# Two of the channel mixing's three parts run during attention instead of one (decaying attention, token and channel mixing, gated convolution; one core)

## The chip, the cores and the metric

The kernel runs on one core of a Trainium2 chip. The metric is the device time of one launch in microseconds: the median of three runs of the kernel before is 717.75 us (716.49 to 718.46). TensorE is called PE here, VectorE DVE, ScalarE ACT, GpSimd POOL and SyncE, which issues the DMAs, SP.

## The reference

Three networks follow one another on 4 batches of 576 positions. The first is causal attention with a decay (8 heads of 64 per batch, 32 heads in all), the second mixes along the positions (token mixing) and then along the channels (channel mixing), the third is a gated convolution.

```python
scores = where(causal, -1e9, q @ k.T / sqrt(64) + decay)     # per head
x = concat_heads(softmax(scores) @ v)                        # [4, 576, 512]
u = x + (relu(x.T @ w_tok1) @ w_tok2).T                      # token mixing, 576 -> 256 -> 576
x2 = u + relu(u @ w_ch1) @ w_ch2                             # channel mixing, 512 -> 1536 -> 512
h = relu(x2 @ w_in)                                          # 512 -> 1024
out = (h * sigmoid(conv3(h))) @ w_out
```

## The kernel before

Every large product is made of three fp16 products: each operand is a high and a low half, and `mm3` (lines 279 to 284) issues high by high, high by low and low by high, so lines 282, 283 and 284 carry nearly all of PE's work. The channel mixing works on 8 chunks of 288 columns, two per batch. Its inner 1536 channels are 12 blocks of 128, called m. For each m, `m1` (w_ch1 by the halves `uh`, `ul` of u) fills a PSUM bank, `rh` on ACT and `rl` on DVE (lines 662 and 666, tile `r`) take it out as two halves, and `m2` (w_ch2 by `r`) sums over m into one bank per output block d.

The 12 blocks are dealt into parts, `PARTS_M = (5, 4, 3)`. The first `EARLY` parts are computed during attention: as soon as a batch's two token mixings are done, part 0 of its two chunks runs, its sum is scaled by ACT (line 682) into the tile `res`, and SP stores it to the DRAM array `p_d`. The other parts run after attention: `mix_input` loads the chunk's halves, u and the stored sum, POOL adds u to the sum (line 739), and DVE adds each later part's bank onto it (line 678).

Weights come as 64-bit numbers. A block goes through the two tiles `wraw`: SP loads it, ACT shifts it (line 319), DVE joins it (lines 323 and 324, the decode), ACT squares it for its size (line 520). A spread on PE (line 262) brings the sizes of a set to all partitions, DVE makes a power of two of them (`pw`), and the set is then split into halves. For an early set `ONP` says by whom: with 2 POOL does it all (line 555 scales, line 274 casts the high half, line 277 makes the low half), with 1 POOL scales and makes the low half and ACT casts, with 0 ACT makes the high half (line 570) and DVE the low one (line 574). Before, w_ch1's part 0 has 2 and w_ch2's part 0 has 0. The sets are called c10 and c20 (w_ch1 and w_ch2 of part 0), c11 and c21 (part 1), c12 and c22 (part 2).

Heads 8 to 30 make the probabilities' halves on POOL (`ph`, line 1037) and DVE (`pl`, line 1043), and a DMA turns each. `pv` multiplies them by v (lines 1098 to 1100; 1093 for the first eight heads), `xh` and `xl` are the halves of a head's result, `t1` and `t2` are the token mixing of four heads. `um` is the size of a batch's u, `su` the power of two made of it, and `ul` (line 613) the low halves that the first m1 needs. Banks of the tag w (four of them) serve spreads, pv, t1, t2, m1 and the early m2.

The order of all this is made on the host: `Order` (line 19) holds tasks with an engine, a duration, a rank, the data they read and write and the banks they take. It always issues what can start first, and of those the lowest rank. The tasks are then emitted in that order, so each engine, SP's queue included, has a fixed program. The early channel mixing has the last rank on PE (`LATE`), so it fills what attention leaves.

Of the kernel before, what the change touches and what calls it, by code (L numbers as in the profile page):

```python
# [8 lines left out]
F32 = mybir.dt.float32  # L9
# [10 lines left out]
class Order:  # L20
# [3 lines left out]
    LAG = {"PE": 0.25, "DVE": 0.12, "ACT": 0.2, "POOL": 0.12, "SP": 0.0, "-": 0.0}  # L24

# [34 lines left out]
    def run(self):  # L60
# [35 lines left out]
        for _ in range(n):  # L96
            best = None
            for e, ks in open_.items():
                if not ks:
                    continue  # L100
                at = free[e] if e != "-" else 0.0
                pick = None
                for k in ks:
                    r = ready[k]
                    if takes[k]:
                        r = max(r, slot(k))
                    if r >= far:
                        continue
                    c = (max(r, at), self.tasks[k][2], k)
                    if pick is None or c < pick:  # L110
                        pick = c
                if pick and (best is None or pick[0] < best[0]):
                    best = (pick[0], pick[2], e)
# [30 lines left out]
def fox_moe_kernel(  # L144
# [14 lines left out]
    nc = tc.nc  # L159
# [51 lines left out]
    XHP = 8  # L211
    ONP, TONP = (2, 0), (1, 1)
    SETR = ((-20.0, 0.0),)
    LATER = (-30.0, 10.0, 30.0)
# [9 lines left out]
    p_d = dram.tile([KD, 128, NT], F32, name="p_d")  # L224
# [418 lines left out]
    def channel_mix(c, part, rank, u_of, p_of, rts, tag, tag2, pe, evac):  # L643
# [40 lines left out]
        def store(d):  # L684
            nc.sync.dma_start(p_d[d, :, c * CH:(c + 1) * CH], box["res", d])
# [12 lines left out]
        for d in range(KD):  # L698
# [14 lines left out]
            T("SP", 0.4, rank + evac, store, d, reads=[kd], writes=[("p_d", c, d)], moved=0.7)  # L713

    def mix_input(c, rank):
# [18 lines left out]
        def load_p():  # L734
            box["p"] = pools["p2a"].tile([128, KD, CH], F32, tag="p", name="p", bufs=PB)
            nc.sync.dma_start(box["p"], p_d[:, :, cols].rearrange("k p s -> p k s"))
# [7 lines left out]
        T("SP", 0.4, rank - 2, load_p, reads=[("p2a",)] + [("p_d", c, d) for d in range(KD)],  # L744
          writes=[(kp, d) for d in range(KD)], moved=2.8)
        T("SP", 0.4, rank - 2, load_u, reads=[("u_d", c, 0), ("u_d", c, 1), ("p2a",)], writes=[ku], moved=2.8)
        for d in range(KD):
            T("POOL", 0.86, rank, add_u, d, reads=[ku], writes=[(kp, d)])
        return (r, kv), (box, kp)
# [17 lines left out]
    with tc.manual_schedule():  # L767
# [277 lines left out]

        def pt_of(n):
# [98 lines left out]
        def pair(p):  # L1145
# [19 lines left out]
            for n in (2 * p, 2 * p + 1):  # L1165
# [17 lines left out]
                else:  # L1183
# [5 lines left out]
                    for q in range(2):  # L1189
                        T("DVE", (1.35, 0.9)[q], rank + 4, lo_part, n, q,  # L1190
# [6 lines left out]
                for i in ORDER:  # L1197
                    T("PE", (0.22 if n < FULL else 0.1) * len(PVB[i]), rank + 6, pv, n, i, reads=[*kp, *vk], writes=[kw, ("xf", g % 2, n % HG)],
                      pools=["a3"], ring=[kw])
                T("DVE", 0.5, rank + 6, norm, n, reads=[kw, ("vsc", g % 3)], writes=[("rs", n % 2)], pools=A1, ring=[kw])  # L1200
                T("DVE", 0.46, rank + 6, xout, n, reads=[kw, ("rs", n % 2)], writes=[("xf", g % 2, n % HG)], pools=A1, ring=[kw])
                T("POOL" if n < XHP else "ACT", 0.47, rank + 6, x_hi, n, reads=[("xf", g % 2, n % HG)], writes=[("xh", n % HG)], pools=A1)
                T("POOL", 1.05, rank + 6, x_lo, n, reads=[("xf", g % 2, n % HG), ("xh", n % HG)],
# [90 lines left out]
        def group(g):  # L1294
            t0 = (HG * g + HG - 1) * PER + 6
# [59 lines left out]
        AVAIL = [(H * (b + 1) - 1) * PER + 30 for b in range(B)]  # L1355
# [31 lines left out]
        for g in range(NG):  # L1387
# [242 lines left out]
```

## Time and profile before

| | |
|---|---|
| median of three runs | 717.75 us |
| the profiled execution | 717.09 us, span 715.3 us |
| PE busy | 693.4 us (97%) |
| DVE, ACT, POOL busy | 501.8, 429.7, 266.2 us |

The busy time of an engine is the union of its instructions. PE is busy nearly everywhere, so what is left to win is its idle time, and the views that list it are the busy time by stretches and the timeline of PE with the idle time that stands ahead of an instruction. Attention lasts until about 300 us, the late channel mixing until about 500 us, and the gated convolution follows.

### The profile page before, as it was taken

The page shows a single profiled execution, that of the slowest core. Times are in us where ns is not written, and L with a number is a line of the kernel's source. Part 1 is how long each engine was busy: PE and PEld are TensorE (multiplying, and loading weights), DVE is VectorE, ACT ScalarE, POOL GpSimd, SP SyncE. Part 2 cuts the span into 40 slices and gives each one's busy share as a digit, 9 for nine tenths or more (in the row PEclk, how much of TensorE's full clock was granted, in tenths as well). Part 3 has the DMA queues.
Part 4 walks back from the last instruction along what each step waited for, and adds up shares of the span by engine and source line. Part 5 has one row for each costly group of instructions (what it writes and reads, how often), then busy time and mean ns, then how long its engine had stood idle before and what let it go on. Part 6 is the DMA issues. An engine that isn't in the chain of part 4 may idle for free.

```text
span 715.3 us, 16400 instructions
## 1 busy us (share of the span) xinstructions
PE 693.4 (97%) x6417; PEld 559.4 (78%) x6417; DVE 501.8 (70%) x1255; ACT 429.7 (60%) x942; POOL 266.2 (37%) x344
## 2 busy tenths in 40 slices
PE   7999897799999999999999999999999999999998
PEld 6888676587778787887888778778878778778786
DVE  5778989998876788436666856635778866875570
ACT  5777886576845685555674544312177766676671
POOL 2145898657682867230000222102023222323240
PEclk9999999999999999999999999999999999999999
DMA  9435899799995987875454855345211121100101
GB/s 203 148 93 176 212 275 186 143 249 244 231 225 123 220 165 178 220 256 157 151 180 124 284 187 164 100 134 160 66 42 58 51 59 35 57 20 26 34 18 51
DMA packets 152974, 101.99 MB, mean 143 GB/s; under 512 B 89984, under 2 KB 145024, under 8 KB 152896
## 3 DMA queue, kind: packets, MB, share of 16 engines
q1 hardware_dynamic: 152896, 100.94, 54.6%
q8 instruction: 50, 0.82, 0.5%
q14 instruction: 28, 0.23, 0.1%
HBM read 57.73 MB, written 23.59 MB: 114 GB/s over the span
## 4 chain that ended last, share of the span: by engine, by line
PE 82%; DVE 7%; POOL 5%; ACT 2%; issue 2%; DMA 1%; SPq 0%; DVEq 0%; POOLq 0%; ACTq 0%
PE w L282 14%; PE w L283 14%; PE w L284 14%; PE z L283 8%; PE z L282 8%; PE z L284 8%; PE z L1004 5%; PE w L1093 3%; PE w L1245 2%; POOL vp L916 2%; PE z L1008 1%; POOL vp L274 1%; DVE pl L1043 1%; ACT t L1028 1%; PE w L1099 1%
## 5 line engine op out<-in xcount | busy, mean ns | idle before, releaser
L284 PEld LDWEIGHTS <-w 128*128 128x128 f16 x1280 | 125.3, 98 | 34.9 <-DVE w L574 3.2
L282 PEld LDWEIGHTS <-w 128*128 128x128 f16 x1280 | 124.9, 98 | 34.4 <-issue 2.7
L283 PEld LDWEIGHTS <-w 128*128 128x128 f16 x1280 | 125.0, 98 | 34.3 <-issue 3.5
L282 PE MATMUL w<-uh,w 128*128 128x288 f16 x416 | 119.0, 286 | 1.2 <-DVE r L666 1.2
L284 PE MATMUL w<-uh,w 128*128 128x288 f16 x416 | 119.0, 286 | 0.0
L283 PE MATMUL w<-ul,w 128*128 128x288 f16 x416 | 119.0, 286 | 0.0
L277 POOL TENSOR_TENSOR g<-sg,g 128x286 f16<-128x286 f32 (+1 forms) x64 | 55.1, 867 | 150.2 <-ACT g L271 148.5
L1530 DVE SCALAR_TENSOR_TENSOR cv<-hp,cw,cv 128x286 f32<-128x286 f32 (+1 forms) x128 | 75.1, 594 | 38.2 <-ACT cv L1524 36.0
L662 ACT ACTIVATE r<-w 128x288 f16<-128x288 f32 x96 | 39.2, 408 | 87.9 <-PE w L284 87.7
L1028 ACT ACTIVATE t<-t,m 128x576 f32<-128x576 f32 (+4 forms) x160 | 81.3, 552 | 17.3 <-DVE m L1022 17.2
L739 POOL TENSOR_TENSOR p<-p,u 128x288 f32<-128x288 f32 x32 | 27.3, 883 | 150.1 <-DVE wraw L323 78.1
L1022 DVE CUSTOM_DVE_ANT_0 t<-z,mask 128x576 f32<-128x576 f32 (+4 forms) x160 | 69.9, 478 | 11.1 <-PE z L1008 11.0
L666 DVE SCALAR_TENSOR_TENSOR r<-w,r 128x288 f16<-128x288 f32 x96 | 43.4, 453 | 47.4 <-ACT r L662 46.6
L283 PE MATMUL z<-g,w 128*128 128x286 f16 (+1 forms) x256 | 73.3, 286 | 0.0
L282 PE MATMUL z<-g,w 128*128 128x286 f16 (+1 forms) x256 | 73.0, 285 | 0.0
L284 PE MATMUL z<-g,w 128*128 128x286 f16 (+1 forms) x256 | 72.9, 285 | 0.0
L284 PE MATMUL w<-vh,w 128*128 128x288 f16 x224 | 64.1, 286 | 0.0
L282 PE MATMUL z<-r,w 128*128 128x288 f16 x224 | 64.1, 286 | 0.0
L283 PE MATMUL w<-vl,w 128*128 128x288 f16 x224 | 64.1, 286 | 0.0
L284 PE MATMUL z<-r,w 128*128 128x288 f16 x224 | 64.1, 286 | 0.0
L282 PE MATMUL w<-vh,w 128*128 128x288 f16 x224 | 64.1, 286 | 0.0
L283 PE MATMUL z<-r,w 128*128 128x288 f16 x224 | 64.1, 286 | 0.0
(206 smaller groups left out, 1699.8 us busy)
## 6 DMA issues: line engine op xcount, KB each, us to landing
wraw<-in_moe_w_ch_dram SPq DMA_DIRECT2D x24, 512.0 KB, 4.7
qk<-in_qk_dram SPq DMA_DIRECT2D x16, 608.0 KB, 5.1
u_d<-us SPq DMA_DIRECT2D x8, 576.0 KB, 4.5
p_d<-res SPq DMA_DIRECT2D x32, 144.0 KB, 3.6
p<-p_d SPq DMA_DIRECT2D x8, 576.0 KB, 5.4
u<-u_d SPq DMA_DIRECT2D x8, 576.0 KB, 4.9
x_d<-p SPq DMA_DIRECT2D x8, 576.0 KB, 3.4
u<-x_d SPq DMA_DIRECT2D x8, 576.0 KB, 3.9
```

What stands on the lines that cost most here:

```text
L277: nc.gpsimd.tensor_tensor(o, a, b, ALU.subtract)
L282: nc.tensor.matmul(ps, wh, xh, start=(first and i == 0), stop=False)
L283: nc.tensor.matmul(ps, wh, xl, start=False, stop=False)
L284: nc.tensor.matmul(ps, wl, xh, start=False, stop=(last and i == n - 1))
L662: nc.scalar.activation(out=t[:, 0, :], in_=box["z", m], func=AF.Relu)
L666: nc.vector.scalar_tensor_tensor(t[:, 1, :], box["z", m], 0.0, f32(t[:, 0, :]), ALU.max, ALU.subtract)
L739: nc.gpsimd.tensor_tensor(box["p"][:, d], box["p"][:, d], box["u"][:, d], ALU.add)
L1004: nc.tensor.matmul(out_[x], t[r, Q0[i]:Q0[i] + 128], t[r, k0:k0 + n], start=first, stop=False)
L1022: nc.vector.tensor_tensor_reduce(to, z_t.pop((n, i)), mk, -0.125, 3e38, ALU.add, ALU.min, m_t[n][0:rows, i:i + 1])
L1028: nc.scalar.activation(out=tt[0:rows, o:o + w], in_=tt[0:rows, o:o + w], func=AF.Exp, bias=m_t[n][0:rows, i:i + 1], scale=-1.0)
L1093: nc.tensor.matmul(o[:, 0:65], p32(n)[:, 128 * blk:128 * blk + 128], vp32_t[g % 2][:, slot, hh, :], start=(j == 0), stop=(j == nb - 1))
L1530: nc.vector.scalar_tensor_tensor(cv, hp_t[m][:, s0 + t:s1 + t], cw[:, t, m:m + 1], cv, ALU.mult, ALU.add)
```

## The change

`PARTS_M` becomes (4, 4, 4) and `EARLY` 2. Parts 0 and 1 of a batch now both run during attention, with ranks 14 apart per chunk, each with its own DRAM array, `p_d[0]` and `p_d[1]`. After attention a third load, `more`, brings the second sum, and POOL adds it in 4 further instructions per chunk. Two further 2 KB weight tiles are kept from the start (NE 17). c11 and c21 are split during attention as the early sets are, c12 and c22 afterwards. Who splits changes: c10 and c11 have 1 (POOL scales and makes low, ACT casts), c20 and c21 have 2 (all on POOL). The token weights' first set is cast by POOL instead of ACT, and so are the high halves of heads 8 to 11 (`XHP`). Ranks of the sets move (`SETR`, `LATER`, `AVAIL`). `WAIT` is 0 for every engine, `REST` is 0, `RG` is 0 and `RN`, `RL`, `RP` are the ranks that stood there before, so the planner's rule and the two new functions for a head's low half change nothing by themselves. In the changed file the helper lines are 8 higher (282 to 284 become 290 to 292) and later ones 20 to 40.

```diff
-    PARTS_M = (5, 4, 3)
-    EARLY = 1
+    PARTS_M = (4, 4, 4)
+    EARLY = 2
-    NE = 15
+    NE = max(15, 2 * M1 + 1)
-    XHP = 8
-    ONP, TONP = (2, 0), (1, 1)
-    SETR = ((-20.0, 0.0),)
-    LATER = (-30.0, 10.0, 30.0)
+    XHP = 12
+    ONP, TONP = (1, 2), (2, 1)
+    SETR = ((0.0, 0.0),)
+    SETR += ((0.0, 45.0),)
+    LATER = (-60.0, 20.0, 40.0)
-    p_d = dram.tile([KD, 128, NT], F32, name="p_d")
+    p_d = [dram.tile([KD, 128, NT], F32, name=f"p_d{x}") for x in range(EARLY)]
...
-            nc.sync.dma_start(p_d[d, :, c * CH:(c + 1) * CH], box["res", d])
+            nc.sync.dma_start(p_d[part][d, :, c * CH:(c + 1) * CH], box["res", d])
...
+        def load_more(x):
+            box["more"] = pools["p2a"].tile([128, KD, CH], F32, tag="more", name="more", bufs=1)
+            nc.sync.dma_start(box["more"], p_d[x][:, :, cols].rearrange("k p s -> p k s"))
+
+        def add_more(d):
+            nc.gpsimd.tensor_tensor(box["p"][:, d], box["p"][:, d], box["more"][:, d], ALU.add)
...
-    AVAIL = [(H * (b + 1) - 1) * PER + 30 for b in range(B)]
+    AVAIL = [(H * (b + 1) - 1) * PER + 20 for b in range(B)]
...
-                for e in range(2):
-                    channel_mix(2 * b + e, 0, AVAIL[b] + e * 14, early_u[2 * b + e], None, rts1, "w", "w", LATE, -20.0)
+                for x in range(EARLY):
+                    for e in range(2):
+                        channel_mix(2 * b + e, x, AVAIL[b] + (e + 2 * x) * 14, early_u[2 * b + e], None, rts1, "w", "w", LATE,
+                                    -20.0)
```

The fixed programs move at three places. The first is POOL where it splits the first weights, at heads 8 and 10 of attention. Before, in POOL's program:

```order
93 L274 TENSOR_SCALAR vp_200<-vf 64x4x64 x2
94 L274 TENSOR_SCALAR vp_200<-vf 128x16x64
95 L916 TENSOR_TENSOR vp_200<-vf,vp_200 64x4x64 x2
96 L916 TENSOR_TENSOR vp_200<-vf,vp_200 128x16x64
97 L277 TENSOR_TENSOR w_113<-w_114,w_113 128x512
98 L1037 TENSOR_SCALAR ph<-t_190 128x1024
99 L274 TENSOR_SCALAR w_114<-w_115 128x512
100 L1037 TENSOR_SCALAR ph<-t_190 128x640
101 L277 TENSOR_TENSOR w_114<-w_115,w_114 128x512
```

The same place now, from the same vp on (w_117 to w_120 are the four blocks of c20, w_116 the last of c10):

```order
96 L936 TENSOR_TENSOR vp_203<-vf,vp_203 128x16x64
97 L563 TENSOR_SCALAR w_118<-w_118,pw_c_231 128x512
98 L563 TENSOR_SCALAR w_119<-w_119,pw_c_231 128x512
99 L563 TENSOR_SCALAR w_120<-w_120,pw_c_231 128x512
100 L285 TENSOR_TENSOR w_116<-w_117,w_116 128x512
101 L563 TENSOR_SCALAR w_121<-w_121,pw_c_231 128x512
102 L282 TENSOR_SCALAR w_117<-w_118 128x512
103 L1057 TENSOR_SCALAR ph<-t_192 128x1024
104 L285 TENSOR_TENSOR w_117<-w_118,w_117 128x512
105 L1057 TENSOR_SCALAR ph<-t_192 128x640
106 L282 TENSOR_SCALAR w_118<-w_119 128x512
107 L1057 TENSOR_SCALAR ph<-t_193 128x1024
```

Before, POOL split only c10 behind the vp and went on to head 10. Now c10 is nearly done there and c20 follows, with head 9's `ph` between. Rows 108 to 116 go on in the same way with two further casts, three further low halves, one `xh`, one `xl`, one scaling of `xf` and one `ph` of 640; row 116 is the low half of the last block, w_120.

The second place is DVE between the batch's size `su` and the first m1. Before:

```order
255 L613 SCALAR_TENSOR_TENSOR ul<-us,su_73,uh 128x576
256 L251 TENSOR_REDUCE pw_c_228<-w 128x1
257 L252 TENSOR_SCALAR pw_c_228<-pw_c_228 128x1
258 L254 TENSOR_SCALAR pw_c_228<-pw_c_228 128x1
259 L255 TENSOR_SCALAR pw_c_228<-pw_c_228 128x1
260 L256 TENSOR_SCALAR pw_c_228<-pw_c_228 128x1
261 L257 TENSOR_SCALAR pw_c_228<-pw_c_228 128x1
262 L613 SCALAR_TENSOR_TENSOR ul<-us,su_73,uh 128x576 x3
```

And now:

```order
252 L331 TENSOR_SCALAR wraw<-wraw 128x512
253 L332 SCALAR_TENSOR_TENSOR w_123<-w_123,wraw 128x512
254 L621 SCALAR_TENSOR_TENSOR ul<-us,su_74,uh 128x576
255 L331 TENSOR_SCALAR wraw<-wraw 128x512
256 L332 SCALAR_TENSOR_TENSOR w_124<-w_124,wraw 128x512
257 L1138 TENSOR_SCALAR rs<-w 128x5
258 L1139 RECIPROCAL rs<-rs 128x5
259 L621 SCALAR_TENSOR_TENSOR ul<-us,su_74,uh 128x576 x2
```

The power of c20 stands earlier now, and two decodes of c11 stand ahead of the first and of the second `ul`.

The third place is the program of PE after the 84 m1 matmuls and two spreads that now open batch 0's channel mixing; before it opened with 108 m1 and one spread, and the first m2 waited for c20's halves from ACT and DVE. In the whole program both kernels have the same matmuls of attention, token mixing, channel mixing and output. Directly ahead of the first m1 PE had, before, 90 matmuls of `pv`, a spread and a score of twelve matmuls behind the spread of `um`; now it has 45 of `pv`.

## Rows read from the trace of the kernel before

**Rows 1.** The page's busy time: us, share of the span, instructions.

```profile
PE 693.4 (97%) x6417; PEld 559.4 (78%) x6417; DVE 501.8 (70%) x1255; ACT 429.7 (60%) x942; POOL 266.2 (37%) x344
```

**Rows 2.** Busy time by stretches: stretch, its length, busy us (instructions) per engine, clock, DMA.

```profile
80.00:100.00 20.00, 16.83 (x136) 13.11 (x135) 17.21 (x48) 16.80 (x35) 19.17 (x25) 1.00 1.02 256
100.00:120.00 20.00, 15.49 (x188) 12.28 (x189) 19.48 (x44) 12.71 (x26) 17.08 (x17) 1.00 1.01 228
120.00:140.00 20.00, 16.19 (x198) 12.59 (x197) 19.07 (x44) 11.35 (x26) 15.08 (x14) 1.00 0.63 131
...
340.00:360.00 20.00, 20.00 (x165) 16.04 (x164) 12.32 (x30) 12.60 (x29) 0.00 (x0) 1.00 0.47 157
```

**Rows 3.** Timeline of PE: start, us, instruction, [idle us ahead, who released it].

```profile
86.99 0.27 PE L283 MATMUL w<-xl,w1h 128*128 128x256 f16 x1 [2.65 <-POOL xl L277]
...
103.17 0.46 PE L262 MATMUL w<-ident,stat_c 128*128 128x128 f32 x2 [0.69 <-DVE rs L1107]
...
106.98 0.30 PE L282 MATMUL w<-uh,w 128*128 128x288 f16 x1
...
113.31 0.46 PE L262 MATMUL w<-ident,vacc 128*128 128x128 f32 x2 [2.48 <-DVE r L666]
...
117.15 0.28 PE L282 MATMUL w<-uh,w 128*128 128x288 f16 x1 [1.18 <-DVE r L666]
...
131.07 0.30 PE L284 MATMUL w<-r,w 128*128 128x288 f16 x1 [2.93 <-DVE w L574]
...
138.63 1.25 PE L1004 MATMUL z<-qk 64*128 64x64 f32 x8 [0.67 <-DVE m L1022]
...
208.10 0.28 PE L282 MATMUL w<-r,w 128*128 128x288 f16 x1 [1.37 <-DVE r L666]
```

**Rows 4.** POOL's groups by line and shape: busy us, mean ns, idle ahead.

```profile
L277 POOL TENSOR_TENSOR xl<-xf,xh 128x320 f16<-128x320 f32 x32 | 30.9, 969 | 56.5 <-ACT xh L271 56.2
L1037 POOL TENSOR_SCALAR ph<-t 128x1024 f16<-128x1024 f32 x23 | 30.1, 1312 | 5.6 <-ACT t L1028 3.7 <-ACT us L1261 1.2 <-DMA pt<-ph 0.6
...
L739 POOL TENSOR_TENSOR p<-p,u 128x288 f32<-128x288 f32 x32 | 27.3, 883 | 150.1 <-DVE wraw L323 78.1 <-DMA p<-p_d 64.5 <-DVE p L678 6.1
L1138 POOL TENSOR_SCALAR xf<-xf,tac 128x320 f32<-128x320 f32 x32 | 23.3, 732 | 1.6
L1037 POOL TENSOR_SCALAR ph<-t 128x640 f16<-128x640 f32 x23 | 21.7, 944 | 2.0 <-ACT t L1028 2.0
...
L277 POOL TENSOR_TENSOR w<-w,w 128x512 f16<-128x512 f32 x5 | 7.3, 1459 | 0.0
...
L274 POOL TENSOR_SCALAR w<-w 128x512 f16<-128x512 f32 x5 | 4.5, 909 | 0.0
L274 POOL TENSOR_SCALAR xh<-xf 128x320 f16<-128x320 f32 x8 | 4.5, 559 | 28.4 <-DVE xf L1116 28.4
L555 POOL TENSOR_SCALAR w<-w,pw_c 128x512 f32<-128x512 f32 x5 | 4.2, 835 | 0.0
```

**Rows 5.** Timeline of POOL at the first weights.

```profile
90.69 1.16 POOL L277 TENSOR_TENSOR w<-w,w 128x512 f16<-128x512 f32 x1
...
96.32 3.59 POOL L916 TENSOR_TENSOR vp<-vf,vp 64x256 f16<-64x256 f32 x3
...
113.93 1.72 POOL L277 TENSOR_TENSOR w<-w,w 128x512 f16<-128x512 f32 x1
```

**Rows 6.** DVE's groups of the decode.

```profile
L324 DVE SCALAR_TENSOR_TENSOR w<-w,wraw 128x512 int32<-128x512 int32 x42 | 33.7, 802 | 5.8 <-ACT w L319 1.5 <-ACT w L570 0.5
...
L323 DVE TENSOR_SCALAR wraw<-wraw 128x512 int32<-128x512 int32 x42 | 19.5, 464 | 0.0
```

**Rows 7.** Timeline of DVE ahead of the first m1.

```profile
98.05 2.41 DVE L324 SCALAR_TENSOR_TENSOR w<-w,wraw 128x512 int32<-128x512 int32 x1 [0.79 <-ACT w L319]
...
103.81 1.70 DVE L613 SCALAR_TENSOR_TENSOR ul<-us,su,uh 128x576 f16<-128x576 f32 x1
...
106.43 3.27 DVE L613 SCALAR_TENSOR_TENSOR ul<-us,su,uh 128x576 f16<-128x576 f32 x3
```

More of the change, by code (lines that the diff above doesn't have):

```diff
@@ L24 @@
     LAG = {"PE": 0.25, "DVE": 0.12, "ACT": 0.2, "POOL": 0.12, "SP": 0.0, "-": 0.0}
+    WAIT = {"PE": 0.0, "DVE": 0.0, "ACT": 0.0, "POOL": 0.0, "SP": 0.0, "-": 0.0}
     def __init__(self, rings):
@@ L101, in run @@
                 at = free[e] if e != "-" else 0.0
-                pick = None
+                starts = []
                 for k in ks:
@@ L106, in run @@
                         r = max(r, slot(k))
[L107 to L113, printed above, removed]
+                    if r < far:
+                        starts.append((max(r, at), self.tasks[k][2], k))
+                if not starts:
+                    continue
+                until_ = min(starts)[0] + self.WAIT[e]
+                pick = min((c[1], c[0], c[2]) for c in starts if c[0] <= until_)
+                if best is None or pick[1] < best[0]:
+                    best = (pick[1], pick[2], e)
             assert best, "the order is stuck: " + str([self.tasks[k][3:5] for ks in open_.values() for k in ks])
@@ L712, in channel_mix @@
             T("ACT", 0.5, rank + evac, copy, d, reads=[kz, back_key], writes=[kd], ring=[kz])
-            T("SP", 0.4, rank + evac, store, d, reads=[kd], writes=[("p_d", c, d)], moved=0.7)
+            T("SP", 0.4, rank + evac, store, d, reads=[kd], writes=[("p_d", part, c, d)], moved=0.7)
     def mix_input(c, rank):
@@ L743, in mix_input @@
             T("SP", 0.4, rank - 4, load_half, x, reads=[("uhl_d", c, x), ("p2a",)] + kv[:x], writes=kv if x == 0 else kv[1:], moved=1.6)
-        T("SP", 0.4, rank - 2, load_p, reads=[("p2a",)] + [("p_d", c, d) for d in range(KD)],
+        T("SP", 0.4, rank - 2, load_p, reads=[("p2a",)] + [("p_d", 0, c, d) for d in range(KD)],
           writes=[(kp, d) for d in range(KD)], moved=2.8)
@@ L748, in mix_input @@
             T("POOL", 0.86, rank, add_u, d, reads=[ku], writes=[(kp, d)])
+        for x in range(1, EARLY):
+            T("SP", 0.4, rank - 2, load_more, x, reads=[("p2a",)] + [("p_d", x, c, d) for d in range(KD)],
+              writes=[("more",)], moved=2.8)
+            for d in range(KD):
+                T("POOL", 0.86, rank, add_more, d, reads=[("more",)], writes=[(kp, d)])
         return (r, kv), (box, kp)
@@ L1189, in pair @@
                     for q in range(2):
-                        T("DVE", (1.35, 0.9)[q], rank + 4, lo_part, n, q,
+                        if n < REST and n % EVERY == 0:
+                            T("POOL", (1.1, 0.75)[q], rank + 4, t_scale, n, q, reads=[("ph", n % 2, q)],
+                              writes=[(*kt, i) for i in SEG[q]], pools=A2)
+                            T("POOL", (2.15, 1.5)[q], rank + 4, lo_rest, n, q,
+                              reads=[(*kt, i) for i in SEG[q]] + [("ph", n % 2, q)], writes=[("pl", n % 2, q)], pools=A2)
+                            continue
+                        T("DVE", (1.35, 0.9)[q], rank + RL, lo_part, n, q,
                           reads=[(*kt, i) for i in SEG[q]] + [("ph", n % 2, q)], writes=[("pl", n % 2, q)], pools=A2)
@@ L1294, in group @@
         def group(g):
-            t0 = (HG * g + HG - 1) * PER + 6
+            t0 = (HG * g + HG - 1) * PER + 6 + RG
             A1 = ["a1"]
```

23 lines of the change are left out of this document (17 added, 6 removed).

## The prediction

> **What bounds the kernel now.** I read the page's busy times first, then the busy time by stretches, then the timeline of PE with its idle times, and only then the groups of POOL and DVE. PE is busy for 693.4 us [rows 1] of a span of 715.3 us, so 21.9 us are idle in all. After attention it is full, for instance 20.00 of 20 us between 340 and 360 [rows 2]. It is not full between 80 and 140, where 3.17, 4.51 and 3.81 us of three stretches are missing, 11.5 us together, more than half of all idle time [rows 2]. That is the time in which the first weights are split and the first batch's channel mixing begins; DVE is then at 17 to 19.5 of 20 us and POOL at 15 to 19. The timeline of PE names the waits [rows 3]: 2.65 us for POOL's `xl`, 2.48 and 1.18 for DVE to empty a bank, 2.93 for the low half of a c20 weight that DVE makes, 0.67 for a score's maximum. Later there is little; the longest I saw is 1.37 us at 208.
>
> So the change can give back at most about what stands in 80 to 140, and it can cost as much as it makes PE wait at any place. The total of matmuls stays the same. A part moved from after attention into it saves no PE time by itself, since PE is full where it comes from and nearly full where it goes.
>
> **The change, part by part.** I follow PE up to the first m2, then what comes after.
>
> First, `xl` of head 7 and the 2.65 us. In the new order POOL starts c10 with four blocks instead of five and makes no casts for it, so this `xl` comes some 3 us earlier by the count of rows ahead of it (two casts at 0.909 and two scalings at 0.835 [rows 4]). But c10's spread on PE now stands ahead of head 7's `pv` and waits for ACT's squares, by my reading of the two orders 1.2 us. I count a gain of 1.4 us here, between 0 and 2.65. It only shows at the next point.
>
> Second, the start of m1. Before it starts at 106.98 [rows 3]. On DVE two decodes now stand ahead of the first two `ul`: 2 x (0.464 + 0.802) = 2.5 us [rows 6]. The power of c20 and the `xf` of a head are gone from there; c20's power took from 105.51 (103.81 + 1.70) to 106.43 [rows 7], 0.9 us, and I put `xf` at half of that. That is +1.1, and the batch's size arrives earlier by part of the 1.4 gained, the rest being lost to ACT's squares: m1 starts at about 106.4, 0.6 earlier. PE has less behind it then: a score and 45 of the 90 `pv` stand later. Before, the score, 30 `pv` and nothing else lie between 103.63 (103.17 + 0.46) and 106.98, 3.35 us [rows 3], and I take 3.2. So at the first m1 the new kernel is 3.2 - 0.6 = 2.6 us behind. Bounds: the decodes could take as long as the one at 98.05, 2.41 us [rows 7], twice, which is 1.6 more for each, 5.8 behind; or hide while ACT makes the high halves, 0.1 behind.
>
> The first m1's run of matmuls: 84 m1 and two spreads, then 9 of the first 12 m2, which need only the first three blocks of c20. A matmul of this kind costs 20.00/165 = 0.121 us [rows 2]: 93 x 0.121 = 11.3, two spreads at most 0.46 each [rows 3], 0.7 together as they overlap, so PE needs the last block of c20 at 106.4 + 12.0 = 118.4 if banks are free.
>
> Third, that last block. POOL's run of `vp` ends at 96.32 + 3.59 = 99.9 [rows 5], and I leave it there, since it waits for v and not for the rows I changed. Behind it stand, up to the low half of w_120, 4 scalings (0.835), 5 low halves (1.459), 4 casts (0.909), 2 `ph` of 1024 (1.312) and 2 of 640 (0.944), one `xh` (0.559), one `xl` (0.969) and one scaling of `xf` (0.732) [rows 4]: 3.3 + 7.3 + 3.6 + 2.6 + 1.9 + 2.3 = 21.0 us, so it ends at 121.0. PE then waits 2.6 us in all between its first m1 and that point, bank waits included, because those fall into the same gap. Before, it waited 2.48 + 1.18 + 2.93 = 6.6 us [rows 3]. Gain 4.0. Bounds: low halves took 1.16 us with DVE out of the way and 1.72 with DVE beside them [rows 5], against the mean of 1.459; scaled by these the 21.0 become 16.7 or 24.8, the end 116.6 or 124.7, and the wait 0 (but about 1 for banks) or 6.3. I take the mean, since it is of the same stretch and the same company.
>
> A rule of the Trainium skill speaks against this part. What the row shows: the decode at 98.05 took 2.41 us instead of 0.802 [rows 6, 7], and it ended 0.5 us after POOL's run of `vp` had ended at 99.9 [rows 5]. The page "SBUF — State Buffer", section "Who interferes with whom", says that a DVE instruction with two SBUF inputs and a GpSimd instruction that reads SBUF take the same port pair as a lock, so that the second to start waits for the whole first. The trace agrees there. By that rule more work on POOL in a dense stretch also lengthens DVE's decodes, `ul` and `pl`, and the sum would move to the slow ends given above.
>
> Fourth, the wait of 0.67 at 138.63 [rows 3], for a maximum that DVE makes: DVE loses its five low halves of c20 just ahead of it, and I count it as gone. It costs 0.67 if not.
>
> Fifth, the rest of attention. Each batch's two chunks now bring 2 x 8 = 16 of the blocks m as filler instead of 2 x 5 = 10, so PE has more to do where a head is late; in exchange POOL has c11 and c21 to split as well: 8 x (0.835 + 1.459) + 4 x 0.909 = 22.0 us [rows 4], which delays the `ph` of heads 10 to 15. DVE saves the low halves of c20, c11 and c21 there. The 1.37 us at 208 is where the first batch's filler ran out; there may be a similar wait at a new place. I count 0 for this part: what hides POOL's 22 us is the filler, and if that cover is gone it is a rival below.
>
> Sixth, after attention: 32 more additions on POOL at 0.883 [rows 4], 28 us, where POOL has 0 of 20 us in a typical stretch [rows 2], and eight more loads; the late m2 that needs the sum stands far behind them in PE's program. Last, c12 and c22 can be loaded only when attention's pool closes, but batch 2's and 3's early parts stand on PE in between, some 40 us of matmuls. Both 0; the end of the kernel is unchanged.
>
> **Sum.** +2.6 - 4.0 - 0.7 = -2.1 us. Against the profiled execution's own 717.1 us that gives 715.0; that execution lies 0.7 under the median of the runs, so on the scale of the median it is 717.75 - 2.1 = 715.6. A change of under 0.3% (2.2 us) can't be told from none here, so this forecast lies on the edge of what can be told: faster below 715.6, slower above 719.9. With the bounds of the single terms it reaches from 711.5 to 721; its own likely range is 713 to 718.
>
> **Rivals.** One: the early stretch closes nearly entirely. For it: the largest single wait is for a DVE low half that no longer exists, and POOL's low halves can take 1.16 us [rows 3, 5]. c20 is then ready at 116.6, before PE asks, which saves 2.6 more, and if the decodes hide as well m1 starts 2.5 sooner: 715.6 - 5.1 = 710.5. Against it: DVE and POOL are both nearly full there.
>
> Two, slower: POOL becomes the engine that PE waits for. It gets 8 x (0.835 + 1.459) + 4 x 0.909 = 22.0 us for c10 and c20 instead of 5 x 3.20 = 16.0 [rows 4], and then 22.0 more behind, in one run from about 75 to 165. If POOL and DVE hold each other up at the slow end (1.72 for 1.459, 18% longer), c20 comes 3.7 later, and over the 22.0 of the following sets 3.9 us more are lost, by which heads 10 to 15 and with them the second batch's channel mixing come late: 715.6 + 7.6 = 723.2. It decides from the point where low halves take more than about 1.6 us on the mean, for then the wait at the first m2 reaches the old one's size and nothing is won to pay for the rest. By the skill's rule this is the likelier side; the rows of the stretch, whose means already hold such company, speak for the middle.
>
> Three: the waits only change places. PE's program is as full as before from 140 on, the missing score and `pv` have to be done later anyway, and 2.1 us is lost to a new wait where the second batch begins: 717.8, no change.
>
> **How the numbers follow.** The forecast has 0.48, and of its range 0.26 lies below 715.6, 0.19 within 0.3% and 0.03 above. Rival one has 0.18, all faster; rival two 0.24, with 0.22 slower and 0.02 within; rival three 0.10, within but for 0.01 slower and 0.01 faster. That makes faster 0.45, same 0.29, slower 0.26. The range for 8 in 10 goes from 709.5, a little beyond rival one, to 723, about rival two; some 2 in 10 lie outside.
>
> **What would show it.** In the new profile: the idle time of PE between 80 and 140 near 9 us instead of 11.5. The wait for DVE's low half of c20 gone and a wait for POOL's low half (now line 285) of 1 to 3 us near 119 in its place. A gap of some 5 us ahead of the first m1, released by DVE's `ul`. DVE's busy time smaller by about the low halves moved, POOL's up by some 60 us (28 for the weights, 44.0 for 16.0, 28 for the additions, and a few casts). PE full from 140 to the end of the kernel. The forecast is wrong if PE shows waits of over 3 us in all between 140 and 330, above all for `pt` or for POOL's weights; wrong on the fast side if the first m2 waits for nothing.

## The result, and the profile after

The changed kernel takes 724.12 us, the median of four runs (721.78 to 724.58), the kernel before on the same chip 717.36 (716.49 to 718.46): ratio 1.0086, 95% interval 1.006 to 1.0113. It is slower, by some 6.8 us, where the forecast said 715.6 and a little faster; the time lies above the forecast's range (709.5 to 723).

The page's busy times after, in the same form as [rows 1]:

```profile
PE 699.3 (97%) x6417; PEld 561.5 (78%) x6417; DVE 488.1 (68%) x1212; ACT 438.2 (61%) x964; POOL 310.1 (43%) x408
```

The span is 722.3 us, so PE is idle for 23.0 us instead of 21.9, and it is busy for 5.9 us more with the same 6417 matmuls. Idle time explains 1 of the 7 us; the matmuls themselves became longer. The busy time by stretches, with the columns of [rows 2] (the granted clock is the third number from the right), says where:

```profile
80.00:100.00 20.00, 16.37 (x128) 11.95 (x126) 18.16 (x56) 15.94 (x36) 18.56 (x25) 1.00 0.79 235
100.00:120.00 20.00, 14.62 (x118) 10.46 (x119) 17.88 (x35) 14.86 (x32) 18.09 (x19) 0.74 0.83 227
120.00:140.00 20.00, 19.66 (x223) 15.46 (x222) 17.15 (x46) 15.34 (x33) 16.68 (x19) 1.00 0.83 216
...
500.00:520.00 20.00, 19.30 (x158) 15.32 (x157) 11.71 (x24) 4.86 (x11) 12.09 (x16) 1.00 0.67 209
520.00:540.00 20.00, 20.00 (x166) 16.08 (x165) 17.75 (x45) 14.66 (x32) 4.00 (x5) 1.00 0.33 94
540.00:560.00 20.00, 17.26 (x129) 13.16 (x128) 18.52 (x43) 13.38 (x32) 6.96 (x9) 0.92 0.17 52
```

Between 80 and 140, 3.63 + 5.38 + 0.34 = 9.35 us are missing instead of 11.5, as forecast for these two traces. But the clock between 100 and 120 is 0.74 on the mean, and behind 500 PE now waits. The kernel before was full there:

```profile
520.00:540.00 20.00, 20.00 (x165) 15.97 (x164) 15.35 (x30) 15.98 (x36) 5.93 (x7) 1.00 0.09 30
540.00:560.00 20.00, 20.00 (x167) 16.08 (x164) 15.32 (x32) 14.39 (x35) 5.86 (x7) 1.00 0.20 61
```

The same view of the changed kernel in finer stretches around the first m1:

```profile
104.00:108.00 4.00, 0.85 (x10) 0.45 (x7) 3.90 (x6) 3.21 (x7) 4.00 (x4) 0.79 0.76 264
108.00:112.00 4.00, 1.77 (x9) 0.95 (x7) 3.86 (x6) 2.69 (x6) 2.78 (x3) 0.50 0.68 208
112.00:116.00 4.00, 4.00 (x19) 2.50 (x18) 4.00 (x7) 2.05 (x5) 3.31 (x3) 0.50 0.97 221
116.00:120.00 4.00, 4.00 (x32) 3.31 (x31) 3.84 (x9) 2.90 (x8) 4.00 (x6) 0.93 1.10 260
```

PE ran for 0.85 of four us, then its clock fell from the upper level (2.4 GHz) to the lower (0.50, 1.2 GHz) and stayed there: between 112 and 116, 19 matmuls fill the four us, later 32. Its timeline there, with the waits in brackets:

```profile
105.14 0.28 PE L290 MATMUL w<-uh,w 128*128 128x288 f16 x1 [0.94 <-ACT uh L618]
107.63 0.40 PE L291 MATMUL w<-ul,w 128*128 128x288 f16 x1 [2.21 <-DVE ul L621]
107.83 0.45 PE L292 MATMUL w<-uh,w 128*128 128x288 f16 x1
...
111.46 0.40 PE L291 MATMUL w<-ul,w 128*128 128x288 f16 x1 [2.23 <-DVE ul L621]
...
557.22 0.80 PE L270 MATMUL w<-ident,xm 128*128 128x128 f32 x2 [2.60 <-DVE xm L276]
```

Two waits for `ul` with six matmuls between them, and far behind them, at 557, a wait for `xm`, the size of one of the gated convolution's input chunks. DVE's timeline shows what stands ahead of each, the decodes of c11:

```profile
104.04 0.80 DVE L331 TENSOR_SCALAR wraw<-wraw 128x512 int32<-128x512 int32 x1
104.94 1.45 DVE L332 SCALAR_TENSOR_TENSOR w<-w,wraw 128x512 int32<-128x512 int32 x1
106.32 1.26 DVE L621 SCALAR_TENSOR_TENSOR ul<-us,su,uh 128x576 f16<-128x576 f32 x1
107.50 0.83 DVE L331 TENSOR_SCALAR wraw<-wraw 128x512 int32<-128x512 int32 x1
108.44 1.33 DVE L332 SCALAR_TENSOR_TENSOR w<-w,wraw 128x512 int32<-128x512 int32 x1
```

I put numbers to the clock as follows: for each slice of 1 us, the busy time of PE times (1 - granted clock), summed; "clock loss" below is this sum, read from one profiled execution. After against before:

| stretch | idle before | idle after | clock loss before | after |
|---|---|---|---|---|
| 0 to 80 | 4.7 | 5.7 | 1.7 | 2.9 |
| 80 to 140 | 11.5 | 9.4 | 0 | 3.4 |
| 140 to 500 | 2.4 | 1.1 | 0 | 0 |
| 500 to 600 | 0 | 3.4 | 0 | 1.5 |
| 600 to the end | 3.4 | 3.4 | 0 | 0 |

Idle +1.1 and clock +6.1 make the 7.0 us of the span, within rounding. By stretch, both together, it is +2.2 up to 80, +1.2 from 80 to 140, -1.3 from there to 500 and +4.9 behind 500: the end of the kernel is the largest part.

This compares one trace with one, and the trace of before is a favourable one. The four executions of the changed kernel had a mean granted clock of 0.985, 0.985, 0.986 and 0.993. The 93 executions of the kernel before that ran beside the experiments had 0.983 to 1.00, 0.993 on the mean; the traced one had 0.998, which 20 of the 93 reach. Span times (1 - clock) is 10.1 us in the changed kernel's trace and 1.4 in that of before, but on the mean 9.2 for the four and 5.0 for the 93. So on the mean the difference in this measure is about half of what the two traces show. It is not lost in full either: the ten of the 93 at a clock of 1.00 took 715.9 us on the mean and the thirteen at 0.988 took 719.5, 3.6 us more for 8.6 us of this measure.

### The profile page after: what moved, and what is told of

It reads as the page before. It is cut to its first block, busy times and chain, and to the rows that moved or that the text cites. A ratio compares the mean times of both kernels' runs of the same rounds, so it can differ in the third digit from the quotient of the medians.

```text
span 722.3 us, 16563 instructions
## 1 busy us (share of the span) xinstructions
PE 699.3 (97%) x6417; PEld 561.5 (78%) x6417; DVE 488.1 (68%) x1212; ACT 438.2 (61%) x964; POOL 310.1 (43%) x408
## 4 chain that ended last, share of the span: by engine, by line
PE 81%; DVE 11%; POOL 4%; ACT 2%; issue 1%; DMA 1%; SPq 0%; DVEq 0%; ACTq 0%
PE w L291 16%; PE w L290 16%; PE w L292 16%; PE z L291 6%; PE z L290 6%; PE z L292 6%; PE z L1024 5%; PE w L1124 2%; DVE w L332 2%; PE w L1282 1%; PE w L1130 1%; PE w L1129 1%; DVE cv L1569 1%; PE w L1131 1%; PE z L1028 1%; DVE t L1042 1%
## 5 line engine op out<-in xcount | busy, mean ns | idle before, releaser
L291 PE MATMUL w<-ul,w 128*128 128x288 f16 x512 | 147.8, 289 | 5.1 <-DVE ul L621 5.1
L290 PE MATMUL w<-uh,w 128*128 128x288 f16 x512 | 147.7, 289 | 0.9 <-ACT uh L618 0.9
L292 PE MATMUL w<-uh,w 128*128 128x288 f16 x512 | 147.9, 289 | 0.0
L1048 ACT ACTIVATE t<-t,m 128x192 f32<-128x192 f32 (+4 forms) x160 | 82.5, 553 | 27.0 <-DVE m L1042 22.6
L1042 DVE CUSTOM_DVE_ANT_0 t<-z,mask 128x192 f32<-128x192 f32 (+4 forms) x160 | 70.7, 479 | 19.7 <-PE z L1028 19.5
L290 PE MATMUL w<-r,w 128*128 128x288 f16 x256 | 73.2, 286 | 0.4 <-DVE pt L1113 0.4
L292 PE MATMUL w<-r,w 128*128 128x288 f16 x256 | 73.2, 286 | 0.0
L291 PE MATMUL w<-r,w 128*128 128x288 f16 x256 | 73.2, 286 | 0.0
L1024 PE MATMUL z<-qk 64*128 64x288 f32 (+4 forms) x384 | 60.1, 426 | 4.8 <-DVE m L1042 2.8
L754 POOL TENSOR_TENSOR p<-p,u 128x288 f32<-128x288 f32 x32 | 25.3, 818 | 91.7 <-DMA p<-p_d 85.4
L1063 DVE SCALAR_TENSOR_TENSOR pl<-t,ph 128x1024 f16<-128x1024 f32 (+1 forms) x46 | 54.6, 1197 | 5.0 <-POOL ph L1057 5.0
L690 ACT ACTIVATE res<-w,backs 128x288 f32<-128x288 f32 x64 | 31.9, 498 | 38.5 <-PE w L292 34.5
```

The source lines that it names most:

```text
L290: nc.tensor.matmul(ps, wh, xh, start=(first and i == 0), stop=False)
L291: nc.tensor.matmul(ps, wh, xl, start=False, stop=False)
L292: nc.tensor.matmul(ps, wl, xh, start=False, stop=(last and i == n - 1))
L690: nc.scalar.activation(out=box["res", d], in_=box["o", d], func=AF.Copy, scale=back)
L1024: nc.tensor.matmul(out_[x], t[r, Q0[i]:Q0[i] + 128], t[r, k0:k0 + n], start=first, stop=False)
L1042: nc.vector.tensor_tensor_reduce(to, z_t.pop((n, i)), mk, -0.125, 3e38, ALU.add, ALU.min, m_t[n][0:rows, i:i + 1])
```

## The experiments

All ratios are against the kernel before on the same chip, with 95% intervals. Theory one: the two decodes keep PE waiting at the first m1, so that the clock falls (3.4 us); and the second early part leaves the gated convolution's inputs late (3.4 idle, 1.5 clock). Rivals stand in each expectation.

**The clock at the first m1.** Matmuls that nobody reads, into the bank that the first m1 then overwrites:

```diff
+            if (c, m, k) == (0, 0, 0):
+                row = wh.rearrange("p k n -> p (k n)")
+                for _ in range(FILL):            # 24; then 44
+                    nc.tensor.matmul(box["z", m], row[:, 0:128], row[:, 0:CH], start=True, stop=True)
```

> The kernel after, with 24 additional matmuls of 128x288 that nobody reads, issued on PE directly ahead of the first m1 (each 0.121 us at full clock, 2.9 us in all), where PE otherwise waits 0.94 and 2.21 us for uh and ul. Theory one (clock): the trace after shows the granted clock at 0.5 from about 106.8 to 116.2, which costs 3.35 us of longer matmuls; with PE busy in that gap the clock stays at 1.00, the first m1 run takes no longer than the idle gaps make it, and the kernel takes about 720.8 us (3.3 less than 724.1). Rival (symptom): what comes behind waits for POOL's last block of c20 at 121.1 or for DVE anyway, so the clock costs nothing: 724, with a wait for L285 of about 3 us at the first m2. Rival (the clock falls from something else than this gap): 724 and still 0.5 in that stretch.

> The kernel after with 44 instead of 24 additional matmuls ahead of the first m1 (44 x 0.121 = 5.3 us). With 24 the wait for the first ul was filled, but PE still waited 2.93 us for the second ul a little later and the clock fell there, costing 1.4 us. Theory one (clock): with 44 the first m1 starts just before the second ul is there, the wait shrinks to about 1 us, the clock between 104 and 116 stays at 1.00, and the first m2 comes some 3 us sooner than in the kernel after: 720.8 us, 1.4 less than with 24. Rival (24 already brought all there was, the rest is noise): 722.2. Rival (the added work delays m1): over 724.

Measured: 1.005 (1.0031 to 1.0068) with 24, 1.0037 (1.0018 to 1.0056) with 44, 720.53 us. The stretches with 44:

```profile
104.00:108.00 4.00, 4.00 (x35) 3.21 (x33) 3.85 (x4) 3.20 (x7) 4.00 (x5) 1.00 0.69 226
108.00:112.00 4.00, 2.98 (x25) 2.24 (x24) 3.91 (x6) 2.70 (x6) 2.39 (x2) 1.00 0.68 208
112.00:116.00 4.00, 3.10 (x26) 2.40 (x25) 4.00 (x7) 3.33 (x9) 3.70 (x3) 1.00 1.24 161
```

With 24 the clock loss was 1.4, behind a remaining wait of 2.93; with 44 it is 0. Work that nobody needs makes the kernel faster (720.5 for 724.1), so the lower clock had a cost of its own, and the rival that a later wait hides all of it falls. But 3.4 us is not what it was worth there: with 44 the stretch from 80 to 140 has 5.95 us idle, no clock loss and 44 x 0.121 = 5.3 us of added matmuls, 11.3 together, against 9.35 + 3.35 = 12.7 without them. That is 1.4 us; the trace also happens to lack the clock loss of 1.5 behind 500. What is left against the kernel before, 0.37%, 2.7 us, is about the idle time behind 500 in this trace (0.39 + 2.75).

The opposite, in the kernel before:

```diff
-            divide(early_u[2 * b + e][0], sl, ..., su[b])[lo]()
+            for _ in range(3 if lo and g < GB and e == 0 else 1):
+                divide(early_u[2 * b + e][0], sl, ..., su[b])[lo]()
```

> The kernel before, in which DVE computes the first two ul of batch 0 three times over (the same result), so that, as in the kernel after behind its two decodes, about 2.2 us more stand ahead of each. Theory (a thin stretch of PE at the first m1 makes the clock fall): waits of some 0.7 and 3.5 us for ul at the first m1, the clock at 0.5 for several us right behind them, 3 to 6 us more than before, ratio 1.004 to 1.009. Rival (the gap is made good by the waits that follow, 2.5 us for r, 1.2 for r and 2.9 for c20's low half, and the clock costs nothing there): ratio 0.998 to 1.003.

Measured: 1.0044 (1.0027 to 1.006). The wait, and the clock behind it:

```profile
112.82 0.40 PE L283 MATMUL w<-ul,w 128*128 128x288 f16 x1 [4.41 <-DVE ul L613]
```

```profile
108.00:112.00 4.00, 0.41 (x4) 0.20 (x2) 3.86 (x7) 0.00 (x0) 4.00 (x4) 1.00 0.51 95
112.00:116.00 4.00, 3.18 (x15) 2.02 (x15) 3.96 (x7) 1.66 (x3) 2.97 (x3) 0.57 0.60 161
```

In this trace the clock fell behind the gap, and part was given back (the wait of 2.48 for `r` [rows 3] was 0.45 here). But the mean granted clock of the seven executions is 0.991, and that of the twelve of the kernel before on the same chip is 0.991 too. So the 0.44% is the price of a longer gap; that it made the clock fall more often is not shown.

**The start, and the gaps of the kernel before.**

```diff
-        for _ in range(11):
+        for _ in range(15):                       # matmuls on the empty mask
```

> As the one before, and with 15 instead of 11 matmuls on the empty mask at the very start, where PE then waits some 2 us for qk and the clock falls in most traces shortly behind (1.7 to 4.5 us of longer matmuls). Theory (the clock at the start falls from that gap): clock at 1.00 in the first 20 us, 718 to 719.5 us. Rival (it falls from the later waits for the first scores' maxima): clock loss at the start as before, 720.8.

> The kernel before with 15 instead of 11 matmuls on the empty mask at the start. Theory (start's clock): 1.5 us less than before, ratio 0.998. Rival (later waits): no change.

Measured: 1.0036 (1.0015 to 1.0057), no better than the 1.0037 without it, and 0.9995 (0.9975 to 1.0016). Both traces have no clock loss in the first 20 us, as expected, but the gain did not show in the medians, nor in the mean clock of the kernel before (0.993 with and without). The second run's trace, in the order of the kernel before, says why one trace is not enough:

```profile
100.00:120.00 20.00, 16.81 (x167) 12.74 (x164) 19.48 (x45) 12.72 (x24) 16.90 (x19) 0.91 1.05 221
120.00:140.00 20.00, 17.07 (x196) 13.15 (x194) 18.42 (x45) 11.79 (x27) 13.80 (x12) 0.91 0.65 130
...
112.00:116.00 4.00, 4.00 (x21) 2.71 (x22) 4.00 (x6) 1.44 (x3) 4.00 (x4) 0.59 1.06 246
124.00:128.00 4.00, 2.66 (x43) 1.91 (x39) 3.59 (x7) 2.42 (x5) 4.00 (x4) 1.00 0.27 54
128.00:132.00 4.00, 2.41 (x21) 1.79 (x22) 3.97 (x11) 1.03 (x3) 1.48 (x2) 0.62 0.98 231
```

The same order lost 3.1 us of clock between 100 and 140, where the trace shown ahead of the prediction lost nothing in the same gaps. So the clock falls in such gaps in some executions and not in others. And where it falls the waits behind it shrink: 3.19 + 2.93 = 6.1 us are idle here, 4.51 + 3.81 = 8.3 in the trace of before [rows 2], so that the fall made this stretch only 0.9 us longer. Filling the gaps:

```diff
+            if (c, part, k) == (0, 0, 0) and m:          # first m1 run: 4 each
+                for _ in range(4): nc.tensor.matmul(box["z", m], row[:, 0:128], row[:, 0:CH], ...)
+            if (c, part, d, m) == (0, 0, 0, 0):           # first m2: 20
+                for _ in range(20): nc.tensor.matmul(box["o", d], ...)
+            if (g, a) == (1, 0):                          # second run only: ahead of t1, 18
+                for _ in range(18): nc.tensor.matmul(st["ps1", a], ...)
```

> The kernel before with 15 instead of 11 matmuls at the start, 4 additional matmuls ahead of each of the blocks 1 to 4 of the first m1 run and 20 ahead of the first m2, into banks that are overwritten, where PE waits 2.5, 1.2 and 2.9 us. Theory (the clock falls in these gaps in part of the runs, as it did in the run with 15 at the start, where it cost 3.1 us): clock at 1.00 all through, 715 us, ratio 0.995 to 0.997. Rival (the added matmuls delay m1 and m2 by as much): ratio 0.999 to 1.002.

> The kernel before with the matmuls that nobody reads of the last run of that kind (15 at the start, 4 ahead of blocks 1 to 4 of the first m1 run, 20 ahead of the first m2) and 18 more ahead of the second group's first t1, where PE waits 2.65 us for xl at 87 and the clock fell in that run (1.7 us). Theory: clock at 1.00 all through in the profiled run, 714.8 us, ratio 0.994 to 0.996. Rival (that fall was rare): no change against 0.9957.

Measured: 715.59 us, 0.9957 (0.9941 to 0.9974), and 715.83 us, 0.998 (0.9962 to 0.9999). Both are faster than the kernel before and the changed one. The mean granted clock of the first is 0.999 against 0.991 of the kernel before on the same chip, so here the added matmuls do keep the clock up, in all six executions; its trace still lost 1.7 us between 80 and 100, where nothing was filled. The cores view of the second, with no fall of the clock at all:

```profile
core 0: 713.9 us, clock 1.000
```

The third place brought nothing that can be told from the first two.

**Who comes first on DVE.** c11's ranks later, alone and with the ring below:

```diff
-    SETR += ((0.0, 45.0),)
+    SETR += ((25.0, 45.0),)
```

> The kernel after, with the ranks of c11 raised from 0 to 25, so that its decodes stand behind the batch's ul on DVE. Theory one (the two decodes make the gap, the gap makes the clock fall): the waits of 2.21 and 2.23 us for ul shrink to under 1 each, the clock between 104 and 116 stays at 1.00, PE comes to the first m2 at about 118 and waits there up to 3 us for POOL's last block of c20 (121.1); 720 to 721 us. Rival (DVE has the same work in any order, so the gap comes back behind): 723 to 725. Rival (c11 comes too late for the second early part): a new wait of several us between 140 and 180, over 725.

> The edits of c11 later and of the ring with three buffers together. If the two losses are independent and both theories hold: 724.1 - 3.4 - 4.9 = about 715.8 us. If only the clock theory of the first gap holds: 720.7; only the late one: 719.2; neither: 724.

Measured: 1.012 (1.0087 to 1.0152) and 1.0124 (1.0093 to 1.0155). The first m1 came 2.5 us earlier, but still waited 2.60 for its first `ul`, and a new wait came with the clock behind it:

```profile
134.86 0.42 PE L290 MATMUL w<-r,w 128*128 128x288 f16 x1 [3.06 <-DVE xf L1147]
```

The rival's mechanism is there: DVE has the same work, and the gap comes back elsewhere. Its time is not: 727.6 us lies above its 723 to 725, and the wait of several us between 140 and 180 that the other rival names is not in the trace either (1.2 us idle from 140 to 200). The traced execution, 724.4, is the fastest of six, so part of the loss is not explained.

**Parts of the change undone.** One early part (EARLY 1, LATER -30, 10, 30), and the old engines for the splits (XHP 8, ONP (2, 0), TONP (1, 1)):

> The kernel after with one early part of four blocks instead of two (EARLY 1; the later sets' ranks as in the kernel before); who splits and the parts 4, 4, 4 stay. No decodes of c11 stand ahead of the batch's ul, and the late channel mixing again has 8 blocks per chunk. Theory (two losses, both from the second early part: the clock in the gap at the first m1, the shorter lead of the gated convolution): clock at 1.00 between 104 and 116, no wait for xm or ul and no clock at 0.5 between 500 and 560; by that 724.1 - 3.4 - 4.9 = 715.8 us. Rival (who splits, POOL instead of ACT and DVE, makes the first loss): the gap of some 5 us and the clock's fall at the first m1 stay, 719. Rival (four blocks are too little filler for attention): over 4 us of new waits between 140 and 300, 720 or more.

> The kernel after with the engines of the splits as before (c10 on POOL, c20 on ACT and DVE, token weights' first set and heads 8 to 11 as before); two early parts stay. On DVE the decodes of c11 then stand behind three of the four ul. Theory: the clock's fall at the first m1 goes (-3.4), the idle time between 80 and 140 comes back from 9.4 to about 11.5 (+2.1), the late loss of 4.9 stays: about 722.8 us. Rival (POOL's splitting is the gain, the clock costs nothing): 726. Rival (second part alone makes all of it): 724.

Measured: 1.0224 (1.02 to 1.0248) and 1.0131 (1.0108 to 1.0153). With one early part of four blocks PE has no waits and no clock loss between 500 and 600, so the late loss comes with the second early part; but attention runs out of filler, 6.8 us idle and 5.5 of clock between 140 and 200, and my sum for it was 18 us too low. With the old engines the late loss stays (5.0 idle, 1.7 clock), and a score's maximum on DVE makes another gap, with its clock (3.0):

```profile
102.89 1.33 PE L1024 MATMUL z<-qk 64*128 64x288 f32 x4 [3.67 <-DVE m L1042]
```

So in the changed kernel POOL's splitting is worth having, and the late loss does not come from it. The gap ahead of the first m1 moved with the engines, so its cause is not settled by this run.

**The late loss.** Four ways to move the gated convolution's inputs. Buffers first: `more` in u's ring with three buffers (e3); as control attention's ring for r, `rts2 = rts1` (e7); with it three buffers for p and u (e8); and three for p with 44 matmuls and 15 at the start (e12):

> The kernel after, with the additional load (more) taken from the ring of u, which gets three buffers instead of two plus one of its own; the same SBUF. The gated convolution's inputs use the same ring. Theory (late): the late channel mixing now has 4 blocks per chunk instead of 7, so the gated convolution's first inputs are loaded about 20 us later and DVE is behind when PE needs them; with a third buffer its inputs come earlier, the waits of 0.70 at 518 and 2.60 at 557 and the clock at 0.5 behind the second go, and the kernel takes about 719.2 us (0.7 + 2.7 + 1.5 = 4.9 less). Rival (DVE's own pile of work between 520 and 556 makes it late, not the buffer): 723 to 724, the wait for xm still there.

> The kernel after, with the late channel mixing's r taken from attention's ring of 9 instead of a ring of its own; it frees 10 KB for the next run and is its control. All theories: as after, 723 to 725 us, with the waits of about 0.7 and 2.6 us behind 500 still there.

> As the control, with three buffers each for the late sum p and for u (two before). In PE's program the first spread of xm then stands 350 rows earlier. Theory (the late loss is lead: p of a chunk waits for the store of the chunk two ahead, that holds u's ring, and u's ring holds the gated convolution's first load, which comes at 505 in the kernel after and at 484 before): the first load comes at 490 or earlier, no wait for xm or ul between 500 and 560, no clock at 0.5 there: 719.2 us (4.9 less). Rival (DVE has too much to do between 520 and 556 whatever the lead): the wait for xm at about 557 stays, 723 to 724.

> The kernel after with the late r from attention's ring, three buffers for the late sum p, 44 additional matmuls ahead of the first m1 and 15 at the start. If the three losses (first gap's clock 3.4, late lead 4.9, start 2) are independent and the shared r ring costs nothing: 724.1 - 10 = 714 us, below the kernel before. If the shared ring's new wait for the sizes of w_out (3 us and the clock behind, seen in its control) stays: 718.

Measured: 1.0163 (1.0133 to 1.0192), 1.0145 (1.0121 to 1.0169), 1.0123 (1.0091 to 1.0155), 1.0083 (1.0052 to 1.0113). The first load of x2 on SP's queue and the wait for xm, of the control:

```profile
510.55 0.50 SPq L635 DMA_DIRECT2D u<-x_d  x1
```

```profile
544.76 0.49 PE L270 MATMUL w<-ident,xm 128*128 128x128 f32 x2 [2.54 <-DVE xm L276]
```

and with three buffers of both:

```profile
491.42 0.51 SPq L635 DMA_DIRECT2D u<-x_d  x1
```

```profile
529.79 0.49 PE L270 MATMUL w<-ident,xm 128*128 128x128 f32 x2 [1.03 <-DVE xm L276]
```

The load comes 19 us earlier and the wait shrinks, with 1.0 us idle between 500 and 600 instead of 2.7; neither trace shows the lower clock there. In e3 the first load came at 508.5 instead of 505.4, later than in the changed kernel, and the idle time there grew to 7.5 with 4.6 of clock. That fits lead. But the times of e7 and e8 can't be told apart: both have new waits between 300 and 500 for the sizes of w_out, and e8 for c12 or c22 too (4.1 and 5.8 us, with 1.6 and 3.3 of clock), since the shared ring moves the order. The same wait, 3.99 us with 2.8 of clock behind it, is in e12. Even with that wait I had expected 718, and it took 724.9: the sum left out the 44 x 0.121 = 5.3 us that the added matmuls take themselves.

Then the other suspects: the third load and the additions left out, with the order kept (the second part's sum is missing from the output); xm planned at 4.0 us, on top of 44 matmuls and 15; and, in the kernel before, the first load made to wait for the last addition of u:

```diff
-            box["more"] = pools["p2a"].tile(...); nc.sync.dma_start(box["more"], ...)
-            nc.gpsimd.tensor_tensor(box["p"][:, d], box["p"][:, d], box["more"][:, d], ALU.add)
+            pass
...
-                T("DVE", 1.3, rank, lambda: largest(xm[c], ubox["u"]), ...)
+                T("DVE", 4.0, rank, lambda: largest(xm[c], ubox["u"]), ...)
...
+        held = [("au", NCH - 1, d) for d in range(KD)] if c == 0 else []
```

> The kernel after with the same order, but the third load and the 32 additions on POOL are left out, so the second part's sum is missing from the output. It prices what the change adds behind attention. Theory (the late loss is lead, not POOL or the loads): 0 to 1 us less than after (724 or a little less), the waits for ul and xm behind 500 nearly as in after. Rival (POOL's additions and the loads make the gated convolution's first inputs late): the first u from x2 comes some 5 us sooner than 505, the waits go, 719 to 720.

> The kernel after with 44 additional matmuls ahead of the first m1 and 15 at the start, and with DVE's reduction xm planned at 4.0 instead of 1.3 us, which puts its spread later in PE's program. Theory (the wait of 2.6 us for xm at 557 is a matter of where the spread stands in PE's order, and PE has matmuls that could run): that wait goes, 717 us, ratio 0.999 to 1.000. Rival (PE's next work needs that xm anyway): the wait moves to a uh or ul, 719.8.

> The kernel before, in which the gated convolution's first load of x2 also waits for the last chunk's addition of u; in the kernel before it is issued at 484, about 35 us before PE's last late matmul, and would come here at about 497, as late against that end as in the kernel after. Theory (lead): waits of 2 to 4 us for xm, uh or ul between 500 and 560 that before doesn't have, and in some runs the clock behind them; 3 to 5 us more than before, ratio 1.003 to 1.007. Rival (the late loss has to do with the shorter late part alone, in which DVE gets less done ahead): no waits, ratio 0.998 to 1.002.

Measured: 1.0057 (1.004 to 1.0073), 1.0073 (1.0054 to 1.0092), 0.9997 (0.9979 to 1.0014). Without the load and the additions the wait is the same:

```profile
555.79 0.49 PE L270 MATMUL w<-ident,xm 128*128 128x128 f32 x2 [2.60 <-DVE xm L276]
```

so they don't make it. The median is some 2 us closer to the kernel before than the changed kernel's, but the intervals overlap, so a small cost of theirs is not excluded. With the spread moved, the wait becomes several, 5.2 us between 540 and 600, two of them

```profile
547.70 0.28 PE L292 MATMUL z<-g,w 128*128 128x286 f16 x1 [0.82 <-POOL g L286]
552.59 0.28 PE L291 MATMUL z<-g,w 128*128 128x286 f16 x1 [1.56 <-ACT o L1601]
```

so moving the spread only moved the waiting. The last one missed its aim: the load came at 488.6, not at 497, and no wait appeared, though the first xm's spread stood 12 us later than before (505.7 for 493.6, in a trace that is 2.5 us longer). It did not test the lead: the load still stood 41 us ahead of the end of the last late m2, against 43 in the kernel before and 24 in the changed one.

Over all the traces this distance goes with the idle time between 500 and 600. With 41 to 48 us (the kernel before, its variants, e5) nothing is idle. With 22 to 27 (the changed kernel and eight of its variants) it is 2.7 to 5.1 us, with 18 (e14) 6.7 and with 16 (e3) 7.5; with 34 (e12) it is 1.4. Only e8 breaks the line, with 50 us and 1.0 idle. That speaks for the lead; no run changed the lead and nothing else.

## Why the prediction was wrong

- **The early idle time** agrees in its sum: -2.1 us forecast, 11.5 to 9.35 in the two traces. That is partly luck. The order of the kernel before, traced in e11 and e17, has 9.4 and 9.0 us idle there, with 3.1 and 4.7 of clock loss. Idle and clock together are 11.5, 12.4 and 13.7 us in the three traces with the order of before, and 12.5 to 12.7 in the five with the changed order (after, e3, e7, e8, e15), so a gain in time is not shown. Of the parts, POOL's last block of c20, forecast for 121.0, ended at 121.14:

```profile
119.98 1.16 POOL L285 TENSOR_TENSOR w<-w,w 128x512 f16<-128x512 f32 x1
```

and the gap at the first m1, "some 5 us", was 0.94 + 2.21 + 2.23 = 5.4. The decodes there took 2.25 and 2.16 us, not 1.27 each, towards the bound that I had given them. But the wait for line 285 near 119 did not come: PE was late itself and reached the first m2 only at 123.8. The wait of 2.65 for `xl` went altogether, but waits of 1.4 for ACT's squares, 0.5 and 0.3 stood in its place, a gain of 0.5 instead of 1.4; and the wait for a score's maximum, counted as gone, was there twice, 1.47 and 0.34.
- **The first step that failed is the sum itself**, which priced a gap at its own length and every matmul at 0.121 us, so that the lower clock behind a gap stood at nothing. I had foreseen the gap and did not ask what PE does behind it: in this trace 9 us at the lower clock, 3.35 us of longer matmuls, which turn the -2.1 us of 80 to 140 into +1.2. In the traces of the four other kernels that keep this order there (e3, e7, e8, e15) it was 3.7 to 3.9; in those of the kernel before, or with its order there (e11, e17), 0 to 3.1. The page "TensorE: Matmul & The Clock Gate" of the Trainium skill, section "HAM oscillation — how this bites in real kernels", warns that waits between bursts of matmuls bring the clock down to half and that this is paid each time. The trace agrees on the half, at 0.50 from 108 to 116. It does not on "each time": the same gaps of the kernel before were followed by it in some traces only.
- **The second is "the end of the kernel is unchanged"**, a term put at 0: it was 3.4 us of idle time and, in this trace, 1.5 of clock, the largest part of the 7.0. I priced what the change adds behind attention (28 us of additions, eight loads) and found it hidden; the wait for xm is the same without it (e15). I did not ask what the shorter late stage takes away: 4 blocks per chunk instead of 7, so the last chunks go through in about 12 us each (96 matmuls of 0.121), and the gated convolution's first load comes at 505 instead of 484, closer to its use. DVE is then busy 17.8 and 18.5 of 20 us between 520 and 560, before 15.4 and 15.3. That the loss comes with the second early part is shown (e5); that the wait is smaller with more lead is seen (e8 against e7, and the distances over all traces); which step of that chain decides is open.
- **Costs and gains of small size**: the wait of 1.37 at 208 went with the fuller filler, a gain of 1.6 between 200 and 300 that I had put at 0. POOL's busy time rose by 44 us, not 60. The first 20 us lost 1.7 more in the changed kernel's trace, 1.2 of them clock, with the same order there; the clock's part varies from trace to trace (0 to 4.5 with 11 matmuls).
- **Rival two** gave 723.2, near the measured time, but not for its reason: POOL is not what PE waits for behind 140, whose idle time up to 500 fell from 2.4 to 1.1.

## What to carry to other kernels

On this engine a gap can have two prices, its length and the clock behind it; the second is paid in some executions only, and later waits can take up a part of it. So it is read from the clock of many executions, and from idle time and clock loss together, not from one trace. Where a gap can't be closed, matmuls into a bank about to be overwritten are a cheap test, and here also the better kernel. When work is moved out of a stage, ask what the next stage prepared beside it.

## What the runs showed of the hardware

The clock's fall is a matter of chance as well as of the gap: the wait of 2.60 for xm was followed by the lower clock in the changed kernel and in e15, and was not in e1, e9 and e10, with the same two engines and the same wait. So a single trace, such as the one of before with no loss between 80 and 140, does not show what a gap costs on the mean. What the executions show is that matmuls in the gaps keep the clock up: 0.999 on the mean in e16, 0.991 without them.
